# Convolution and routed experts on one core: blocks of 512 rows with seven products for eight, and whole sequences routed at once

## The chip, the cores and the metric

The kernel runs on one core of one Trainium2 chip. The metric is the device time of one execution in microseconds. Times of several runs are given as their median; one further execution is taken by the hardware profiler, and views of the profile come from that one. The engines are called TensorE (PE; its weight loads are PEld), VectorE (DVE), ScalarE (ACT), GpSimd (POOL) and SyncE (SP).

## The reference

A light convolution of 8 sequences of 3584 tokens with 192 channels (8 heads of 24, seven taps, softmax over the taps) feeds a mixture of 8 experts of width 1024. A token goes to the expert with its largest logit, unless a local gate says that it stays with the expert of the token before it, so the routing is a scan along the sequence:

```python
out = np.einsum('hk,bskhg->bshg', w, x_unf)          # causal, 7 taps
...
logits = np.einsum('bsd,de->bse', x, w_gate)
local_gate = 1.0 / (1.0 + np.exp(-np.einsum('bsd,de->bse', x, w_local).squeeze(-1)))
...
            if s == 0 or local_gate[b, s] < 0.5:
                e = fresh_e
            else:
                e = prev_e if prev_e >= 0 else fresh_e
...
            h = np.maximum(x[b, s] @ w1[e], 0.0)
            out[b, s] = p[e] * (h @ w2[e])           # p: softmax of the logits
```

Everything is fp32. Each token goes through one expert: a first product 192 to 1024, a relu, a second product 1024 to 192.

## The kernel before, in words

The 28,672 tokens are 16 groups of 1792 (`PT`), two groups to a sequence. Groups 0 and 1 take a path of their own at the start (`wide`, `wide_route`), on TensorE. A later group is loaded with its halo by `load_x` (one transfer of 1.9 MB on SP's queue), convolved on VectorE by `conv` (L366: per head one ACT scaling and six VectorE multiply-adds, L387, over 128 x 336 elements), and routed by `route` (L601): `logits` (L565) turns the rows on VectorE (L570) and multiplies on TensorE (L580), and some ninety small VectorE instructions find each token's expert and its slot in DRAM. `put` (L768) scatters 128 rows at a time to their slots with an indirect transfer on GpSimd's queue (L775).

The slots of an expert are units of 128 rows. `table` (L788) makes a list on the chip of units that are already full, and the static list `blocks` (L887) says which entry of which table a block takes: 35 blocks of one unit, 87 of two, 20 of one, and two spare ones at the end that are entered by a test on the chip. The caps `ONE` and `TWO` come from `_sure` (L48): only as many blocks are planned after a group as must be full whatever the routing.

A block loads its expert's weights (`load_w`, 1.5 MB, SP's queue, four buffers, three blocks ahead) and its rows (`load_rows`), turns the rows on TensorE into PSUM and copies them out on ACT (`turn`, L928, L949), and computes the first product with relu (`hidden`, L952; matmuls L963, ACT L968) and the second (`output`, L973; matmuls L980). The second product's sum is scaled by the token's probability on ACT (L988) and VectorE (L992), and an indirect transfer writes the rows to the output (L996). The contraction over 192 channels is cut into three pieces of 64 rows, and the width of 1024 into two halves, one in each half of TensorE's rows; an fp32 matmul of the code shows as two records.

The order of the work is written out by hand. The loop over `blocks` (L1138) issues for each block `hidden`, the turning of the next block's rows, `step`, `output`, `step`. `step(time)` (L1037) issues VectorE work of convolution and routing for about `time` microseconds by the costs that the generators yield. PSUM has four one-bank buffers for the first product, two for the second and one of two banks for the turned rows.

## Time and profile before

| | us |
|---|---|
| median of 3 runs | 1315.88 (1315.37 to 1316.42) |
| the profiled execution | 1326.81 |
| its span, first to last instruction | 1325.1 |
| TensorE busy (share of the span) | 1304.4 (98%) |
| VectorE busy | 778.3 (59%) |
| ACT busy | 625.2 (47%) |
| GpSimd busy | 480.4 (36%) |
| second product on TensorE, L980, 7328 records | 641.0 |
| first product on TensorE, L963, 6816 records | 637.2 |
| convolution on VectorE, L387, 672 instructions | 376.5 |
| moved by DMA | 325.29 MB |

A group of instructions is named by its line, engine and operation, with what it writes and reads; its busy time is the time in which at least one of its instructions ran, so overlapping matmuls are not counted twice. A wait is put down to the instruction that released it. The timeline gives the start and the length of runs of like instructions.

### The profile page before, as it was taken

The numbers are of one execution on the slowest core, as the hardware profiler recorded it, in microseconds if no ns is written. First come the engines' busy times: TensorE is split into PE (matmuls) and PEld (weight loads), VectorE is DVE, ScalarE is ACT, GpSimd is POOL, SyncE is SP. The second block draws the span as 40 slices with busy tenths as digits, with TensorE's granted clock in tenths as the row PEclk, the third lists the DMA queues.
The fourth block names the chain that finished last, engine by engine and source line by source line (L and its number), as shares of the span: only waits on it lengthen the run. The fifth ranks groups of instructions, "written<-read, shape, count | busy, mean of one in ns | idle before, by whom it ended". The sixth has DMA issues, their size and how long they took to land. (4 is left out here: it accounts for less than half of the span.)

```text
span 1325.1 us, 41356 instructions
## 1 busy us (share of the span) xinstructions
PE 1304.4 (98%) x16682; PEld 1260.9 (95%) x16682; DVE 778.3 (59%) x2434; ACT 625.2 (47%) x1571; POOL 480.4 (36%) x520
## 2 busy tenths in 40 slices
PE   9899999999999999999999999999999999999997
PEld 7799999999999999999999999999999999999997
DVE  6888898977878787878777878785610000000000
ACT  5345555544454545444545454544444444444553
POOL 4445352534343434343434343434344212211111
PEclk9999999999999999999999999999999999999999
DMA  5789999967575757575757575756565555556893
GB/s 188 283 349 391 376 365 345 394 213 266 182 275 177 290 188 277 201 260 192 271 186 273 193 271 199 267 195 210 197 211 205 189 185 188 192 187 229 313 317 131
DMA packets 67298, 325.29 MB, mean 245 GB/s; under 512 B 12576, under 2 KB 38103, under 8 KB 47650
## 3 DMA queue, kind: packets, MB, share of 16 engines
q1 hardware_dynamic: 44784, 277.41, 58.4%
q0 software_dynamic: 22320, 45.22, 9.2%
q8 instruction: 133, 2.18, 0.7%
q14 instruction: 59, 0.48, 0.1%
q10 hardware_dynamic: 2, 0.00, 0.0%
HBM read 277.29 MB, written 45.77 MB: 244 GB/s over the span
## 5 line engine op out<-in xcount | busy, mean ns | idle before, releaser
L980 PE MATMUL yps<-wb,hT 64*128 64x192 f32 x7328 | 641.0, 325 | 5.8 <-ACT hT L968 2.8
L963 PE MATMUL hps<-xT,wb 64*128 64x256 f32 (+1 forms) x6816 | 637.2, 336 | 1.7 <-issue 1.4
L963 PEld LDWEIGHTS hps<-xT,wb 64*128 64x128 f32 x6816 | 589.1, 187 | 27.2 <-issue 4.0
L980 PEld LDWEIGHTS yps<-wb,hT 64*128 64x128 f32 x7328 | 602.8, 187 | 11.1 <-issue 4.6
L996 POOL DMA_INDIRECT out_dram<-o_sb,xg x229 | 232.3, 1014 | 605.7 <-DVE o_sb L992 533.9
L968 ACT ACTIVATE hT<-hps 128x512 f32<-128x512 f32 (+1 forms) x568 | 261.9, 512 | 361.4 <-PE hps L963 246.5
L387 DVE SCALAR_TENSOR_TENSOR y_sb<-x_sb,c,y_sb 128x336 f32<-128x336 f32 x672 | 376.5, 570 | 18.9 <-issue 0.8
L992 DVE SCALAR_TENSOR_TENSOR o_sb<-yps,xg,o_sb 128x192 f32<-128x192 f32 x229 | 87.5, 414 | 467.8 <-ACT o_sb L988 461.4
L775 POOL DMA_INDIRECT slots<-y_sb,posi x228 | 231.2, 1014 | 209.3 <-ACT xT L949 114.8
L988 ACT ACTIVATE o_sb<-yps,xg 128x192 f32<-128x192 f32 x229 | 86.9, 418 | 289.8 <-PE yps L980 287.4
L949 ACT COPY xT<-xps 64x256 f32<-64x256 f32 (+4 forms) x568 | 210.8, 371 | 11.7 <-issue 1.7
L377 ACT ACTIVATE y_sb<-x_sb,c 128x336 f32<-128x336 f32 x112 | 63.7, 581 | 0.0
L359 PEld LDWEIGHTS xps<-ident,xg 64*128 64x128 f32 (+1 forms) x916 | 57.0, 124 | 5.2
L359 PE MATMUL xps<-ident,xg 64*128 64x64 f32 (+1 forms) x916 | 60.0, 217 | 0.0
L570 DVE STREAM_TRANSPOSE z<-y_sb 128x768 f32<-128x768 f32 (+1 forms) x56 | 45.4, 853 | 0.4
L596 DVE COPY lt<-lq 32x36 f32<-32x36 f32 x224 | 40.8, 182 | 3.5
L580 PE MATMUL hps<-z,wg 64*32 64x128 f32 x1344 | 24.2, 272 | 1.2 <-issue 1.2
L580 PEld LDWEIGHTS hps<-z,wg 64*32 64x32 f32 x1344 | 19.2, 105 | 4.1 <-issue 2.9
L556 PE MATMUL yps<-y_sb,hot 112*128 112x194 f32 x64 | 12.6, 353 | 1.4 <-DVE hot L550 1.1
L556 PEld LDWEIGHTS yps<-y_sb,hot 112*128 112x128 f32 x64 | 11.3, 202 | 2.1 <-DVE hot L550 1.6
L672 DVE COPY bk<-so_far 1x32 f32<-1x32 f32 x56 | 12.3, 220 | 0.7
L588 DVE STREAM_TRANSPOSE lq<-ls 128x256 f32<-128x256 f32 x14 | 6.2, 441 | 10.9 <-ACT ls L585 10.9
(236 smaller groups left out, 358.0 us busy)
## 6 DMA issues: line engine op xcount, KB each, us to landing
wb<-in_w_dram SPq DMA_DIRECT2D x138, 1536.0 KB
x_sb<-in_x_dram SPq DMA_DIRECT2D x14, 1920.0 KB
xg<-slots SPq DMA_DIRECT2D x87, 195.0 KB
wb<-in_w_dram SPq DMA_DIRECT2D x12, 512.0 KB
xg<-slots SPq DMA_DIRECT2D x53, 97.5 KB
out_dram<-o_sb,xg POOLq DMA_INDIRECT x229
slots<-y_sb,posi POOLq DMA_INDIRECT x228
x_sb<-in_xb_dram SPq DMA_DIRECT2D x4, 768.0 KB
```

What stands on the lines that cost most here:

```text
L359: nc.tensor.transpose(to, src[rows], identity=ident[rows, rows])
L377: nc.scalar.activation(cols(h), chans(h, 0), Act.Copy, scale=c[:, h, 0:1])
L387: nc.vector.scalar_tensor_tensor(cols(h), chans(h, k), c[:, h, k:k + 1], cols(h), Alu.mult, Alu.add)
L570: nc.vector.transpose(z[:, t:u, :], y_sb[:, t:u, Y0:Y0 + D])
L775: ins = nc.gpsimd.indirect_dma_start(out=slots[:, :], in_=rows, in_offset=None, out_offset=bass.IndirectOffsetOnAxis(ap=to, axis=0)).ins
L949: copied = nc.scalar.copy(a, b)
L963: nc.tensor.matmul(hps[half][:, j, w], lhsT=wb[rows, f0:f0 + P], rhs=xT[rows, d, w], start=(d == 0 and j == 0), stop=(d == KD - 1), skip_g ...
L968: relu = nc.scalar.activation(hT[:, m:m + 2, w], hps[half][:, :, w], Act.Relu)
L980: nc.tensor.matmul(yps[half][:, k * D:(k + 1) * D], lhsT=hT[rows, m, k * P:(k + 1) * P], rhs=wb[rows, WA + m * D:WA + (m + 1) * D], start= ...
L988: nc.scalar.activation(o_sb[:, k, :], y[k][0], Act.Copy, scale=xg[:, k, 0:1])
L992: nc.vector.scalar_tensor_tensor(o_sb[:, k, :], y[k][1], xg[:, k, 0:1], o_sb[:, k, :], Alu.mult, Alu.add)
L996: sent = nc.gpsimd.indirect_dma_start(out=out, in_=o_sb[:, k, :], in_offset=None, out_offset=bass.IndirectOffsetOnAxis(ap=xg.bitcast(I32)[ ...
```

## The change

**Blocks.** The static list becomes 51 blocks of one unit, 20 of two, 31 of four (512 rows) and 14 of one. A new estimate, `_likely`, plans blocks that are full for a routing as it is expected; where an entry of a table is not full, the block takes a unit of padding, and 28 spare blocks, in two nested tests, take what is then left.

**Seven products.** For a block of 512 rows the first product takes two of its three pieces of channels as a 2 x 2 by 2 x 2 block product (rows in halves of 256, the width in two halves) and forms it with Strassen's seven products (`seven`); the third piece is added with four plain ones. GpSimd forms the combined weights (`combine_w`, four subtractions of 128 x 256), VectorE the combined rows (`combine_x`, five), and partial sums go from PSUM through ACT copies and VectorE adds to `h11`, `h12`, `h21`, `h22`. The second product of such a block is done in two parts of 256 rows.

**Convolution and routing.** From group 4 on two groups, a whole sequence, are convolved and routed together (`GROUPS`, `NS`), and x lies by heads: a unit of convolution is one head of one group or sequence, with its own load (240 or 417 KB) on ACT's queue, begun by `taps` behind the scaling of the output.

**Logits.** The group of logits matmuls is cut in two, and the first half stands inside the second product of a block (`visit`), at the earliest one block after the turning; before, the whole group stood ahead of it.

**The rest.** Scatters hang behind other steps and one at a time, PSUM is cut in four pools of two banks, buffers of the start lie in a pool that is closed before the blocks, and the start has another order.

```diff
-ONE = [_sure(min(g + 1, EARLY) * PT, UT) for g in range(NPART)]
-TWO = [_sure((g + 1) * PT - ONE[-1] * UT, BT) if g >= EARLY else 0 for g in range(NPART)]
+def _likely(tokens, size, left):
+    return max(0, (tokens - left) // size)
...
+GROUPS = [*range(EARLY)] + [*range(EARLY + 1, NPART, 2)]
+ONE = {g: _sure((g + 1) * PT, UT) if g + 1 < EARLY else _likely(EARLY * PT, UT, LEFT1) for g in GROUPS}
...
+FOUR = {g: _likely((g + 1) * PT - PAST, QT, LEFT if g < LAST else LEFT3) if g + 1 >= FIRST else 0
+        for g in GROUPS}
...
+        x_sb = x_all[:, at:at + n + HALO, :]
+        src = x[g // PER, qq]
...
+        (queue or nc.scalar).dma_start(out=x_sb.rearrange("p t d -> p (t d)"), in_=win)
...
+            load_x(u)
+        for u in range(max(st["unit"], 0), st["unit"] + 4):
+            if u > st["unit"] and not ready(u, wait):
+                return
+            if u not in begun and most:
+                tap(u)
+                most -= 1
...
+        for k in range(1, KC):
+            nc.vector.scalar_tensor_tensor(cols, x_in[u][:, k:k + n, :],
+                                           c[:, h, k:k + 1], cols, Alu.mult, Alu.add)
+            yield 0.6 if n == NT else 1.0
...
+            for b in range(DQ):
+                if b == DQ // 2:
+                    yield "half"
...
+    def combine_x(xT):
+        xc = hp.tile([P, 4, HU * P], F32, name="xc")
+        one, two = slice(0, HU * P), slice(HU * P, KT * P)
+        nc.vector.tensor_tensor(xc[:, 0, :], xT[:, 0, one], xT[:, 0, two], op=Alu.subtract)
+        nc.vector.tensor_tensor(xT[:, 0, two], xT[:, 0, two], xT[:, 1, two], op=Alu.add)
...
+    def seven(wb, wt, xT, xc, turn_next, weights_next):
...
+        def times(to, a, b, first=False):
+            for j in range(2):
+                for half, rows in halves():
+                    ins = nc.tensor.matmul(to[:, half, j, :], lhsT=b[rows, j * P:(j + 1) * P],
+                                           rhs=a[rows, :], start=(first and j == 0), stop=True,
+                                           skip_group_check=True)
+            return ins
+
+        times(xb, a11, b11, True)
+        nc.scalar.copy(h11, xb)
+        times(yb, s1, t1, True)
+        times(yb, a23, b32)
+        nc.scalar.copy(h22, yb)
+        times(xb, s2, t2)
+        nc.scalar.copy(h12, xb)
+        put(times(wbk, a12, b21, True))
+        times(wbk, a13, b31)
+        step(SIDE[0], None, 1)
+        nc.vector.tensor_tensor(h11, wbk, h11, op=Alu.add)
+        nc.scalar.activation(h11, h11, Act.Relu)
+        put(times(xb, s3, t3))
+        nc.vector.tensor_tensor(h22, xb, h22, op=Alu.add)
+        nc.scalar.activation(h22, h22, Act.Relu)
+        times(yb, s4, b22)
+        put(times(yb, s5, b32))
+        at = turn_next()
+        times(xb, a22, t4)
+        wt = weights_next()
+        next(wt)
+        put(times(xb, a23, b31))
+        next(wt)
+        nc.vector.tensor_tensor(h12, yb, h12, op=Alu.add)
+        nc.scalar.activation(h12, h12, Act.Relu)
+        nc.scalar.activation(h21, xb, Act.Relu)
+        return [[h11, h12], [h21, h22]], at, wt
...
+    SIDE = (2.8, 4.4, 1.6, 1.4)
...
-    step(1.8)
-    xT, _ = turn(blocks[0][1], xgs[0])
-    gather(1, ya, picks[1], range(9, NB))
+    puts_behind(mark["rs", 1], 4)
+    at = turn_out(blocks[0][1], xgs[0])
+    xgs[1] = gathered(picks[1])
+    xT, _ = turn_in(blocks[0][1], at)
     next(route1)
-    puts_behind(mark["oh", 1], 2)
-    step(2.4)
-    xgs[1] = gathered(picks[1])
+    step(0.6)
```

## The prediction

> **What bounds the kernel now.** I read the busy table and the slices first, then TensorE's timeline in steady state, then the stretches, then the waits. In the page, the slices are busy tenths of each engine over 40 equal parts of the span:
>
> ```profile
> PE   9899999999999999999999999999999999999997
> DVE  6888898977878787878777878785610000000000
> PEclk9999999999999999999999999999999999999999
> DMA  5789999967575757575757575756565555556893
> ```
>
> TensorE is full from the second slice to the end at full clock; VectorE has nothing left to do after two thirds of it. DMA is full in slices 4 to 8. So TensorE's own work sets the time, and the question is what a block of it costs. Its timeline, start and length in us, first for blocks of 256 rows, then of 128, then with a logits group between:
>
> ```profile
> 1102.37 5.34 PE L963 MATMUL hps<-xT,wb 64*128 64x256 f32 x48
> 1107.55 0.39 PE L359 MATMUL xps<-ident,xg 64*128 64x64 f32 x8
> 1107.78 5.42 PE L980 MATMUL yps<-wb,hT 64*128 64x192 f32 x64
> 1113.03 5.34 PE L963 MATMUL hps<-xT,wb 64*128 64x256 f32 x48
> ...
> 1263.88 2.84 PE L963 MATMUL hps<-xT,wb 64*128 64x128 f32 x48
> 1266.56 0.28 PE L359 MATMUL xps<-ident,xg 64*128 64x64 f32 x4
> 1266.67 2.82 PE L980 MATMUL yps<-wb,hT 64*128 64x192 f32 x32
> 1269.33 2.84 PE L963 MATMUL hps<-xT,wb 64*128 64x128 f32 x48
> ...
> 329.95 0.56 PE L359 MATMUL xps<-ident,xg 64*128 64x64 f32 x8
> 330.44 1.59 PE L580 MATMUL hps<-z,wg 64*32 64x128 f32 x96
> 331.96 5.74 PE L980 MATMUL yps<-wb,hT 64*128 64x192 f32 x63
> ```
>
> From start to start: a 256-row block takes 10.66 us (48 records at 107.9 ns, 8 transposes at 28.8, 64 records at 82.0); each fp32 matmul of the code is two records. A 128-row block takes 5.445. The logits group starts 0.26 after the transposes' 0.23 us are over and holds TensorE until 331.96: 1.78 us.
>
> The stretches (busy us and, in brackets, instructions; then clock, DMA share, GB/s) show where TensorE is not full:
>
> ```profile
> 50.00:100.00 50.00, 45.48 (x727) 43.38 (x726) 41.63 (x130) 25.44 (x80) 22.39 (x23) 1.00 0.82 314
> 100.00:150.00 50.00, 48.55 (x789) 47.02 (x788) 44.61 (x117) 27.10 (x84) 25.40 (x26) 1.00 1.01 399
> 150.00:200.00 50.00, 49.58 (x749) 48.94 (x748) 44.59 (x145) 27.51 (x88) 20.99 (x20) 1.00 0.95 356
> 1000.00:1100.00 100.00, 100.00 (x1134) 93.87 (x1134) 6.68 (x18) 42.98 (x96) 27.23 (x28) 1.00 0.57 198
> ```
>
> The ledger from the starts of the blocks: the 35 single blocks run 46.16 to 260.09, 213.9 us, against 35 x 5.445 + 4 logits x 1.78 = 197.7 of work: 16.2 lost, 5.5 of it in the first four blocks, 10.7 (0.34 each) in the other 31, where DMA stands at 0.95 to 1.01 [...]. The 87 pairs run to 1208.90, 948.8 us against 927.4 + 10 x 1.78: 3.6 lost. The last 20 singles lose 0.5. The wait table agrees: TensorE's own named waits come to some 13 us, ACT's, VectorE's and GpSimd's to hundreds, which cost nothing while TensorE is full.
>
> [...]
>
> **The change part by part.** Which blocks run follows from the constants: before 35 singles, 87 pairs, 20 singles; after 51 singles, 20 pairs, 31 fours, 14 singles. Both are 229 units of 128. Routing the reference's own inputs by its own rule gives 229 units and fills each planned block, so neither the two spare units of before nor the 28 of after are entered, and no block of padding runs.
>
> 1. Strassen. A block of 512 is 11 calls of `times`, each 4 matmuls or 8 records of 256 columns: 88 x 107.9 = 9.50 us; 16 transposes 0.46; second product 128 x 82.0 = 10.50. Sum 20.46, against 2 x 10.66 = 21.32: 0.86 less, x31 = **-26.7 us**.
> 2. Five pairs become ten singles: 54.45 - 53.3 = **+1.15**.
> 3. Logits: still 14 groups of 96 records, each now in two halves: [...] 14 x 0.26 = **+3.6**. [...]
> 4. The single stage is 16 longer at the same appetite for weights (1.5 MB per 5.445 us is 289 GB/s, rows in and out add 36, x and scatters the rest of the 355 to 399 measured). At 0.34 each: 16 x 0.34 = +5.4. In front of it the two slices of convolution (1.8 and 2.4) leave VectorE's path to `oh` and `upto`, and block 2's rows, whose scatters end at 52 now, can be fetched some 2 us sooner: -2. Together **+3.3**; from -8 (loads of 240 KB in place of one of 1.9 MB no longer collide with weights) to +15 (twice the loss).
> 5. Stalls inside a block of 512. Its eviction is a chain TensorE, ACT, VectorE, TensorE. I price ACT from its rows (256 elements 381 ns, 512 595, so 1024 about 1.02 us) and VectorE's add from `oh` (112, 275 ns) and `hot` (512, 691): 1024 about 1.22, an estimate with a PSUM operand taken at the same rate. From the block's start: call 1 ends 0.86, ACT copies h11 to 2.1, h22 to 3.85, h12 to 4.9; call 7 wants that bank at 5.2: 0.25 spare. VectorE adds h11 5.4 to 6.6, h22 6.6 to 7.8; the call after the transposes wants it at 8.23: 0.3 spare. h12 is ready at 10.4 for 12.6, h21 at 11.4 for 15.2. Behind the ACT copies stand o_sb's scalings and the taps, behind the adds the convolution slices of VectorE, whose five subtractions for the next block (5 x 0.425) end at 19.1 and are wanted at 21.3. So the margins hold but thinly: 0 to 0.9 a block, I take 0.15: +4.7. The 20 pairs lose 0.8; before lost 3.6. Net **+1.9**.
> 6. The first block of 512 has its weights combined in a row and its rows after that: once, **+1.5** (0 to 3).
>
> Costed at nothing: convolution by heads. VectorE's rows give 192 elements 414 and 336 elements 570 ns, so 672 about 0.93: 96 x 0.57 + 288 x 0.93 = 323 us against 376.5; routing two groups at once saves more, the adds and subtractions cost 31 x 5.8 = 180. VectorE ends near 810 us busy, in a block of 512 about 17.7 of 20.46 (10.2 of planned slices, 5.8, four scalings 1.7); the cover is TensorE's time, and without it each us late shows. GpSimd per block of 512: 4 sends, 6 scatters at 1.0 and 4 subtractions of some 0.75 are 13 of 20.5. ACT issues x's loads, 64 of them (SP's take 0.33 us); in a single block ACT has the second half of TensorE's time free, and relu waits if a tap and a load come together. Where the scatters were spread, they still wait on TensorE's or ACT's steps; GpSimd alone waits. The gathers' buffers, the pools opened anew and the tables touch no engine at its limit. The tail after the last matmul, 1318 to 1325, stays.
>
> Sum: -26.7 + 1.15 + 3.6 + 3.3 + 1.9 + 1.5 = -15.2. The profiled execution took 1326.81 with a span of 1325.1; the span becomes 1309.9. It was 0.8% above the median of the runs, 1315.88; I carry the difference over: **1300.7**.
>
> **The rivals.** (a) The front clears: small x loads leave the weights on time, the single stage loses 8 in all and blocks of 512 nothing. That is 11.5 and 4.7 better than my sum, less what the pairs lose anyway: about 1287. For it: half of the loss sits where a 1.9 MB load ran. Against: 399 GB/s is the measured ceiling, and it is reached for 50 us. (b) Slower: the chain in the block of 512. If call 7 waits for ACT's copy and the call after the transposes for VectorE's add, 0.45 each, a block loses 0.9 and not 0.15: 31 x 0.75 = +23, 1324. It decides from 0.64 a block on. For it: spare times of 0.25 and 0.3 in two strict queues that carry other work; against: the work ahead in them is sliced to end before. (c) The DMA front is worse: at 0.66 a single the 47 later blocks lose 31, not 16: 1316, no change. For it: share 1.01 already; against: x's halo shrinks from 20/14 to 34/28 of the rows. (d) The seven products do not save TensorE time, if 44 matmuls go slower than 48[...].
>
> **How the numbers follow.** Mine 0.52 (1294 to 1308), (a) 0.20 (1284 to 1294), (c) 0.15 (1308 to 1318), (b) 0.13. Within 0.2% is 1313.3 to 1318.5, about what a measurement can tell from no change. Faster: 0.52 + 0.20 + half of (c) = 0.80; same 0.07; slower 0.13. The range 1287 to 1319 leaves out most of (b) and the best of (a).
>
> **What would show it.** Right: blocks of 512 start 20.5 to 20.8 us apart, with 88 records near 108 ns; the first block of 256 starts near 350 us; 28 logits bursts. Wrong: idle of TensorE before the first product named after ACT's copies or VectorE's adds (b); single blocks 6 us apart with DMA at 1.0 (c); singles at 5.45 throughout (a). Blocks of 512 above 21.3 apart would overturn the forecast.

## The result, and the profile after

| | before | after |
|---|---|---|
| median of the runs, us | 1315.62 (1314.50 to 1316.42) | 1330.73 (1325.88 to 1331.05) |
| the profiled execution, us | 1326.81 | 1330.98 |
| its span | 1325.1 | 1329.3 |
| TensorE busy | 1304.4 | 1285.1 |
| VectorE, ACT, GpSimd busy | 778, 625, 480 | 821, 691, 618 |
| moved by DMA, MB | 325.29 | 281.17 |

The changed kernel is slower: the ratio is 1.0107, with an interval of 1.0082 to 1.0131. The forecast was 1300.7, so it went the other way. TensorE is busy for 19 us less, and still the end comes later. (A set is the runs that were made together; the same program before took 1315 us in four of the six sets and 1329 to 1332 in the other two, so times are compared within a set only.)

The page of the changed kernel, the slices of the span that answer to those shown of before:

```profile
PE   8879999999899999989999999899999999999997
DVE  6857888789678898885788955853333334333100
PEclk9999999999999999999999999999999999999999
DMA  4888999989877678664434434335334333233483
```

Before, TensorE's row was 9 in slice 1 and from the third slice on. Now it has an 8 in slice 1, a 7 in slice 3, and 8s in slices 11, 18 and 26, and VectorE's row has gained work to the end. The DMA row is at 8 or 9 from slice 2 to 11, where before has that from 3 to 8, and far emptier behind. The wait table of TensorE in the same execution (releaser, us in total, times, longest) names what the gaps wait for:

```profile
PE ps L400 <- DVE h L1140: 8.1, 3, 3.5
PE ps L1170 <- DVE o_sb L1186: 7.6, 2, 5.9
PE ps L1170 <- ACT h L1078: 3.8, 1, 3.8
PE ps L1125 <- DVE xT L1103: 3.2, 2, 2.6
PE ps L400 <- DMA xg<-slots: 3.1, 1, 3.1
```

Four of the five releasers are VectorE or ACT. The prediction had put the waits inside a block at 4.7 us in all and the convolution on VectorE at nothing. A block of 512 without a wait is as predicted; the timeline of TensorE (start, length) has:

```profile
886.20 10.58 PE L1170 MATMUL ps<-wb,h 64*128 64x192 f32 x128
896.60 2.77 PE L1125 MATMUL ps<-xT,wb 64*128 64x256 f32 x24
...
904.37 0.65 PE L400 MATMUL ps<-ident,xg 64*128 64x64 f32 x16
...
906.62 0.67 PE L1170 MATMUL ps<-wb,h 64*128 64x192 f32 x6
```

From second product to second product 906.62 - 886.20 = 20.42 us; the prediction had 20.46. Of the 30 distances from one such block to the next, 20 are 20.41 to 20.43 us, and seven, where logits stand or VectorE is busy with routing, 20.5 to 23.5. Most of the loss is in three blocks: the first (25.96), the second (23.04) and the thirteenth, at 846.78 (29.40). The thirteenth waits twice for VectorE, as TensorE's timeline shows, and VectorE's has routing (L912) right up to the add (L1140) that ends the second wait:

```profile
850.42 2.00 PE L1125 MATMUL ps<-xT,wb 64*128 64x256 f32 x16 [2.58 <-DVE xT L1103]
861.09 0.69 PE L400 MATMUL ps<-ident,xg 64*128 64x64 f32 x16 [3.49 <-DVE h L1140]
```

```profile
859.67 0.23 DVE L912 SCALAR_TENSOR_TENSOR inn<-ends,pf,inn 128x8 f32<-128x8 f32 x1
859.82 1.22 DVE L1140 TENSOR_TENSOR h<-ps,h 128x1024 f32<-128x1024 f32 x1
```

The ledger by stages, from the starts of the blocks in this execution. Work is blocks times their undisturbed length (5.445, 10.66, 20.42) and half logits bursts at 1.09:

| stage | starts, us | took | work | lost | lost, as predicted |
|---|---|---|---|---|---|
| before the first block | 0 | 42.98 | | | 46.2 at the start, as before |
| 51 singles | 42.98 | 318.5 | 290.8 | 27.7 | 19.6 (16.2 + 5.4 - 2) |
| 20 pairs | 361.46 | 222.3 | 221.9 | 0.4 | 0.8 |
| 31 of 512 | 583.77 | 659.8 | 641.7 | 18.1 | 6.2 |
| 14 singles | 1243.6 | 76.3 | 76.2 | 0 | 0.5 |
| tail behind the last matmul | 1319.86 | 9.4 | | | 6.8 |

In the front, the loss is not spread over the singles. 33 of the 51 take 5.44 or 5.45 us from start to start, and of the other 18 six hold the two half bursts of a group of logits; the loss is at a few places. The first twelve singles lose 18.4 of the 27.7 us, and the last one, at the handover to the pairs, 5.2. Two of the places, in the timelines of ACT and then TensorE:

```profile
69.20 0.34 ACTq L156 DMA_DIRECT2D x_sb<-in_x_dram  x1
...
80.27 0.58 ACT L425 ACTIVATE y_sb<-x_sb,c 128x336 f32<-128x336 f32 x1 [5.21 <-DMA x_sb<-in_x_dram]
80.75 1.18 ACT L1078 ACTIVATE h<-ps 128x256 f32<-128x256 f32 x4
...
85.49 0.36 ACTq L156 DMA_DIRECT2D x_sb<-in_x_dram  x1
...
95.77 0.58 ACT L425 ACTIVATE y_sb<-x_sb,c 128x336 f32<-128x336 f32 x1 [5.79 <-DMA x_sb<-in_x_dram]
...
96.38 0.42 ACT L1180 ACTIVATE o_sb<-ps,xg 128x192 f32<-128x192 f32 x1
```

```profile
77.08 0.31 PE L400 MATMUL ps<-ident,xg 64*128 64x64 f32 x4
81.17 4.26 PE L1170 MATMUL ps<-wb,h 64*128 64x192 f32 x32 [3.78 <-ACT h L1078]
...
88.16 2.87 PE L1170 MATMUL ps<-wb,h 64*128 64x192 f32 x32
...
99.75 5.20 PE L1170 MATMUL ps<-wb,h 64*128 64x192 f32 x32 [5.93 <-DVE o_sb L1186]
```

ACT stands at a scaling of x (L425) whose load is still under way, and the relu (L1078) and the scaling of the output (L1180) stand behind it in ACT's queue; TensorE waits for these. Counted in the order of the loads, the first scaling needs the one issued at 69.20, the second the one at 85.49: 11.1 and 10.3 us for 240 KB. The lengths in TensorE's lines show a second price: 32 records take 4.26 and 5.20 us behind the two stalls and 2.87 without one.

### The profile page after: what moved, and what is told of

Read it like the earlier page. It is cut to its first block, busy times and chain, and to the rows that moved or that the text cites. A ratio compares the mean times of both kernels' runs of the same rounds, so it can differ in the third digit from the quotient of the medians.

```text
span 1329.3 us, 40917 instructions
## 1 busy us (share of the span) xinstructions
PE 1285.1 (97%) x16674; PEld 1237.7 (93%) x16674; DVE 821.3 (62%) x1891; ACT 691.1 (52%) x1402; POOL 618.4 (47%) x650
## 2 busy tenths in 40 slices
DMA packets 67395, 281.17 MB, mean 212 GB/s; under 512 B 12544, under 2 KB 33207, under 8 KB 52866
## 4 chain that ended last, share of the span: by engine, by line
PE 50%; DVE 3%; ACT 1%; issue 0%; POOL 0%; POOLq 0%; DVEq 0%; ACTq 0%
PE ps L1170 26%; PE ps L1125 20%; PE ps L1074 3%; PE ps L400 1%; DVE y_sb L461 1%; PE ps L662 1%; ACT xT L1052 0%; DVE h L1143 0%; DVE o_sb L1186 0%; DVE h L1140 0%; DVE h L1153 0%; ACT h L1154 0%; ACT h L1134 0%; ACT y_sb L425 0%; ACT h L1136 0%
## 5 line engine op out<-in xcount | busy, mean ns | idle before, releaser
L1170 PE MATMUL ps<-wb,h 64*128 64x192 f32 x7328 | 632.3, 326 | 11.8 <-DVE o_sb L1186 7.6
L1170 PEld LDWEIGHTS ps<-wb,h 64*128 64x128 f32 x7328 | 603.4, 189 | 17.1 <-ACT xT L1052 7.9
L461 DVE SCALAR_TENSOR_TENSOR y_sb<-x_sb,c,y_sb 128x672 f32<-128x672 f32 (+1 forms) x384 | 321.9, 847 | 52.8 <-ACT y_sb L425 42.7
L1074 PE MATMUL ps<-xT,wb 64*128 64x128 f32 (+1 forms) x4080 | 295.3, 297 | 3.4 <-issue 1.9
L1074 PEld LDWEIGHTS ps<-xT,wb 64*128 64x128 f32 x4080 | 275.6, 188 | 16.6 <-issue 3.7
L1186 DVE SCALAR_TENSOR_TENSOR o_sb<-ps,xg,o_sb 128x192 f32<-128x192 f32 x229 | 87.2, 410 | 274.3 <-ACT o_sb L1180 273.0
L1180 ACT ACTIVATE o_sb<-ps,xg 128x192 f32<-128x192 f32 x229 | 87.3, 418 | 312.4 <-PE ps L1170 311.1
L1078 ACT ACTIVATE h<-ps 128x256 f32<-128x256 f32 (+1 forms) x340 | 128.6, 431 | 146.0 <-PE ps L1074 119.5
L1052 ACT COPY xT<-ps 128x128 f32<-128x128 f32 (+2 forms) x464 | 194.1, 418 | 9.8 <-PE ps L400 3.2
L1125 PE MATMUL ps<-xT,wb 64*128 64x256 f32 x1488 | 179.9, 379 | 3.2 <-DVE xT L1103 3.2
L1125 PEld LDWEIGHTS ps<-xT,wb 64*128 64x128 f32 x1488 | 154.1, 189 | 10.2 <-issue 3.9
L1140 DVE TENSOR_TENSOR h<-ps,h 128x1024 f32<-128x1024 f32 x31 | 37.9, 1222 | 77.4 <-PE ps L1125 77.3
L1125 PE MATMUL ps<-xc,wt 64*128 64x256 f32 x496 | 64.8, 376 | 0.0
L425 ACT ACTIVATE y_sb<-x_sb,c 128x672 f32<-128x672 f32 (+1 forms) x64 | 50.8, 796 | 18.2 <-DMA x_sb<-in_x_dram 14.9
L1125 PE MATMUL ps<-xc,wb 64*128 64x256 f32 x496 | 59.2, 376 | 0.0
L400 PE MATMUL ps<-ident,xg 64*64 64x64 f32 (+1 forms) x916 | 47.4, 218 | 11.1 <-DVE h L1140 8.1
L400 PEld LDWEIGHTS ps<-ident,xg 64*64 64x64 f32 (+1 forms) x916 | 42.7, 123 | 16.3 <-DVE h L1140 9.3
```

The source lines that it names most:

```text
L400: nc.tensor.transpose(to, src[rows], identity=ident[rows, rows])
L425: nc.scalar.activation(got[g][:, :, Y0 + h * GS:Y0 + (h + 1) * GS], x_in[u][:, :n, :], Act.Copy, scale=c[:, h, 0:1])
L461: nc.vector.scalar_tensor_tensor(cols, x_in[u][:, k:k + n, :], c[:, h, k:k + 1], cols, Alu.mult, Alu.add)
L1052: copied = nc.scalar.copy(a, b)
L1074: nc.tensor.matmul(hps[:, half, j, :], lhsT=wb[rows, f0:f0 + P], rhs=xT[rows, d, :], start=(d == 0 and j == 0), stop=(d == KD - 1), skip_g ...
L1078: relu = nc.scalar.activation(hT[two][:, half], hps[:, half], Act.Relu)
```

## The experiments

**Set 1: the kernels again, and two single edits.** The first two runs are the unchanged kernels.

> The kernel before, unchanged, for a profile of it at its usual time: the one shown took 1326.81, the timed runs 1315.6. If the 11 us lie in the single blocks, [...] the first block of 256 rows starts near 249 and not at 260.09; if they are spread, all blocks are longer.

> The changed kernel, unchanged: 1326 to 1331. If its stalls are fixed by its order, TensorE's waits for ACT's relu near 81 us, for VectorE near 100 and near 861 are there again, within 1 us of the lengths 3.8, 5.9 and 3.5; if they come from chance in the transfers, they move or go.

Before took 1326.11 us (one run; the set's other runs of it have a median of 1329.36), with its first 256-row block at 259.89: no execution near 1315 was seen in this set, so the question stayed open. The changed kernel took 1357.76, ratio 1.0205 (1.0176 to 1.0234). Its stalls are at the same places: blocks of 512 of 25.96, 24.63 and 29.40 us (first, second, thirteenth), ACT's late scalings with TensorE stalls of 4.83 and 5.13 in the first twelve singles. That is the order of the work. What is larger is above all the single stage, 333.3 us against 318.5. The second block, 24.63 here and 23.04 before, is taken up in the last section.

```diff
-        if st["unit"] + 1 == len(UNITS) and st["cgen"] is None:
-            time *= 1.6
```

> The factor of 1.6 on each slice of VectorE's side work after the last convolution is taken out; nothing else. Theory of the queues (routing slices are issued ahead of the adds that TensorE waits for): the block that starts near 847 falls from 29.3 us to 20.4, and the time by 8 to 9 us, to 1322. Rival (the blocks of 512 wait for something else, such as transfers): the block stays long and the time within 2 us of 1330.7.

Measured 1353.57, 1.0180 (1.0152 to 1.0208) beside 1.0205: 3 to 4 us for the 8 to 9 expected, and the two intervals overlap. The thirteenth block does fall from 29.40 to 20.42 us, as expected. But the last group is now routed later, and another wait takes its place, in TensorE's timeline of this kernel:

```profile
1014.56 1.94 PE L1125 MATMUL ps<-xc,wb 64*128 64x256 f32 x16
1022.50 1.12 PE L400 MATMUL ps<-ident,xg 64*128 64x64 f32 x16 [6.00 <-DMA xg<-slots]
```

The block that turns here is the first that needs rows of the last two groups. The stretch paid 9 us early for rows in time; without it 6 us come back later, with longer records behind them (the eight that take 2.05 us take 1.14 in the changed kernel's second block of 512, at a granted clock of 1.00).

```diff
-        if st["cgen"] is None and ready(st["unit"] + 1):
+        if st["cgen"] is None and ready(st["unit"] + 1, 3 if st["block"] < 21 else 1):
```

> In the first 21 blocks a convolution unit may begin three blocks after its load was issued, not one; no work is taken out. Theory of the queues (ACT stands at a scaling whose x has not landed, and the relu behind it is late): the ACT waits of 5.2 and 5.8 us and TensorE's of 3.8 and 5.9 go, and the time falls by 10 to 15 us, to 1318. Rival (weights and x are short of bandwidth whatever waits for them): TensorE waits as long for weights, time within 3 us of 1330.7.

Measured 1357.92, 1.0211 (1.0185 to 1.0236): no gain, the rival's number. Yet the rival's reason is not what the trace shows. ACT's waits for x fell from 10.8 us to 3.5 and both stalls in the first twelve singles are gone; the stage of single blocks is 322.7 us against 333.3 in the run beside it. The time came back as TensorE waiting for rows, 8.9 us in three places, one of them in the pairs:

```profile
494.80 0.69 PE L400 MATMUL ps<-ident,xg 64*128 64x64 f32 x8 [4.29 <-DMA xg<-slots]
```

VectorE may start each unit only later, so routing, scatters and then rows are late; that this is the way from the edit to the late rows is read from the order of the work and was not tested apart. Here the wait moved off ACT came back as a wait for rows.

**Set 2: which part of the change loses.** Before takes 1314.84 in this set. The changed kernel itself was not run in it: where before takes 1315 it was at 1.0107 in the result and at 1.0047 in set 3, so a gain or loss of a few us beside it can't be read from the times of this set.

```diff
-        times(xb, a11, b11, True)
-        nc.scalar.copy(h11, xb)
...
+        def three(to, parts, weights):
+            for k in range(3):
+                ins = times(to, parts[k], weights[k], k == 0)
+            return ins
...
+        three(xb, lefts, ones_)
+        nc.scalar.activation(h11, xb, Act.Relu)
+        put(three(yb, lefts, twos_))
+        nc.scalar.activation(h12, yb, Act.Relu)
```

> The changed kernel with the first product of a block of 512 as twelve plain products (96 records in place of 88), without the combined weights and rows and without VectorE's adds: each quarter of h is made by one ACT relu from PSUM. Same output. By the prediction's first step a block costs 8 x 107.9 ns = 0.86 us more, 26.7 us over 31 blocks; but the stalls that wait for VectorE's adds and subtractions (some 15 us in the changed kernel's blocks of 512) should go. Theory, both hold: 8 to 15 us slower than the changed kernel on the same chip (1357.8 there), blocks 21.3 us apart, stage of blocks of 512 near 672 us. Rival, the stalls come from the convolution's place in VectorE's queue and stay: 22 to 27 us slower. Rival, the seven products' helpers (adds, subtractions, copies) take back all they save: within 3 us.

1335.58, 1.0165 (1.0148 to 1.0182). In the timeline the first product of such a block is one unbroken run of 96 records:

```profile
865.57 10.53 PE L1104 MATMUL ps<-xT,wb 64*128 64x256 f32 x96
875.92 0.63 PE L400 MATMUL ps<-ident,xg 64*128 64x64 f32 x16
```

A block takes 21.28 us, 0.86 more than 20.42, exactly the 8 x 107.9 ns of the prediction. The 31 blocks take 668.0 us (580.32 to 1248.32), which is 31 x 21.28 and the logits with nothing lost. So both halves of the theory hold: the seven products save 26.7, and the 18.1 lost in the changed kernel's blocks belong to what they need from the other engines. The edit takes out VectorE's part, GpSimd's and ACT's copies together; it is the wait table that names VectorE. The net gain of the seven products as made is 668.0 - 659.8 = 8 us.

```diff
-FIRST = 8
-PAIRED = 20
+FIRST = 16
+PAIRED = 99
```

> The changed kernel without blocks of 512: 51 blocks of one unit, 81 of two, 16 of one. Same output. What is left of the change is its front, its convolution by heads, the sequences routed whole and the logits in halves. Theory: the blocks of 512 do gain, 26.7 less some 17 of stalls, so this is 8 to 15 us slower than the changed kernel and 35 to 45 above the kernel before on this chip (1329), all of it in the single blocks, the logits and the tail. Rival, blocks of 512 are where the loss is: at least 5 us faster than the changed kernel.

1345.79, 1.0220 (1.0173 to 1.0267), beside 1.0047 to 1.0107 for the changed kernel where before takes 1315. The rival falls: blocks of 512 are no net loss. What stays of the change without them costs some 30 us.

```diff
-PAIRED = 20
+PAIRED = 28
...
-ONE = {g: ... else _likely(EARLY * PT, UT, LEFT1) for g in GROUPS}
+ONE = {g: ... else _sure((EARLY - 1) * PT, UT) for g in GROUPS}
-BT, LEFT2)) if g >= EARLY else 0
+BT, LEFT2)) if g >= EARLY else 8 if g == EARLY - 1 else 0
```

> The changed kernel with the 16 single blocks of group 3 made into 8 pairs: 35 singles, 28 pairs, 31 blocks of 512, 14 singles. Same output; 8 loads of weights of 1.5 MB fewer in the front. Theory A, the loss in single blocks is a loss per single ([...] 42 us over 51 in the changed kernel on this chip, 28 on the other): 16 x 0.5 to 0.8 plus 8 x 0.23 of work = 10 to 15 us faster than the changed kernel on the same chip. Theory B, the loss is at two places in the first twelve singles (x landing late for ACT) and at the handover: 2 to 5 us faster.

1335.63, 1.0146 (1.0121 to 1.0170): no faster, contrary to both theories. (The profiled execution, 1342.05, is the slowest of its four.) But it speaks against theory A. The 35 singles now take 222.0 us (43.17 to 265.15), 22.7 more than their work, and 19.2 of these lie in the first twelve, as 18.4 do in the changed kernel. The loss is not per single. The eight pairs behind them then run into a wait that the wait table puts first:

```profile
PE ps L400 <- DMA xg<-slots: 14.8, 1, 14.8
PE ps L400 <- DVE h L1140: 6.4, 3, 2.9
PE ps L1170 <- DVE o_sb L1186: 6.2, 1, 6.2
```

The rows of groups 4 and 5 come at 362, when all blocks made of the first four groups are done. In the changed kernel the same rows come at 357. TensorE can't pass that point early, whatever the front saves, for a whole sequence must be convolved, routed and scattered first.

```diff
-    for u in range(4):
+    for u in range(6):
         load_x(u, nc.sync)
...
-        for _ in range(most):
+        for _ in range(2):
             u = len(x_in)
```

> The changed kernel with x loaded earlier: six units ahead of the first block in place of four, and up to two loads per single block in place of one (no more than six in flight, as now). Same output and same bytes. Theory B, x arrives at one unit per single block while VectorE could convolve 1.4, so ACT's scalings wait for x and what stands behind them is late: ACT's waits for x go, TensorE's two stalls of 4 to 6 us near 80 and 100 us go with the slow clock after them; 8 to 15 us faster than the changed kernel on the same chip. Theory A, the transfers themselves are the limit: the same bytes land no sooner, weights come late in their place; within 3 us.

1324.80, 1.0072 (1.0052 to 1.0093). The 8 to 15 us that were expected are not shown, since the changed kernel's own 1.0047 to 1.0107 lie on both sides. Beside the kernel with twelve products, which has the changed kernel's front and ran in this set, the single stage is 3.0 us shorter, 311.1 for 314.1. The stall near 100 us (1.9 us there, 5.9 in the result's execution) is gone, the one near 80 stands with 3.1, and the handover still waits 3.6 us for rows. ACT's scalings wait 4.9 us for x by name, and 5.9 us are put down to transfers of weights (4.5 of it at the scaling near 80). Theory B holds in kind and not in size: the same bytes, begun earlier, end part of the waits.

**Set 3: the mends together.** Before takes 1315.60.

> The changed kernel as it is, for the comparisons of this set: 1.1% above the kernel before on a chip where that takes 1315, as in the result; stalls at the same places in the blocks of 512 (first block 25.9 us, second 23.0, the block near 847 us 29.3), since these come from the order of VectorE's work and not from the transfers. Rival, the places shift: then the stalls are chance meetings.

1322.52, 1.0047 (1.0030 to 1.0063), and not the 1.1% that was expected. The stalls in the blocks of 512 are where they were, 25.83, 23.03 and 29.25 us: no chance meetings. Those of the front are at their places too, near 80 and 97 us, but at 2.8 and 2.4 us they are shorter than the result's 3.8 and 5.9, and the single stage is 312.6 us for 318.5. So the loss in the blocks of 512 repeats, and the loss in the front does not have a fixed size.

```diff
-PAIRED = 20
-LEFT1 = 640
+PAIRED = 19
+LEFT1 = 384
-LEFT = 2900
+LEFT = 1876
...
-        for _ in range(most):
+        for _ in range(2):
...
-        if st["unit"] + 1 == len(UNITS) and st["cgen"] is None:
-            time *= 1.6
...
-    for u in range(4):
+    for u in range(6):
...
-            if spot and part == 0:
-                taps(min(n, 2), 2 if n == 1 else 1)
+            if spot is not None and part == 0:
+                taps(min(n, 2) if spot else 0, 2 if n == 1 else 1)
...
-        if n < KT:
+        if n < KT and not n < n_next == KT:
             step(1.4 if n == 1 else 3.6)
```

> The changed kernel with what the runs so far name: six units of x loaded ahead and two per block (7 us in the run with earlier loads); 53 single blocks and 19 pairs in place of 51 and 20, so that the first pair comes 10.7 us of work later and finds its rows (5 us less at the handover, 0.2 more work); no convolution step at the end of the last pair block, but its loads of x (3 to 7 us of the 8 in the first two blocks of 512); no stretched steps after the last convolution, with two more blocks of 512 planned ahead of the last group so that its rows are not wanted at once (8 us, and not the 6 us wait for rows of the run without the stretch alone). Theory, each stall has its own place and cause: the sum is -18 to -27, 1304 to 1313 where before takes 1315. Rival, a stall that is removed comes back elsewhere, as in the two runs with one edit each: -7 to -10, the earlier loads' own gain.

1301.70, 0.9894 (0.9877 to 0.9910) of before, 20.8 us under the changed kernel in the same set. The 31 blocks of 512 take 641.7 us (571.87 to 1213.61): their work and nothing else. That is 17.8 of the 25.7 by which the two profiled spans of this set differ (1324.2 and 1298.6). The single stage takes 316.7 for 53 singles, 6.8 less than the changed kernel's 312.6 plus the 10.9 of two more; and TensorE's named waits are now

```profile
PE ps L1170 <- ACT h L1078: 3.3, 1, 3.3
PE ps L1170 <- DVE o_sb L1186: 1.6, 2, 1.0
PE ps L1170 <- ACT xT L1052: 1.5, 1, 1.5
...
PE ps L400 <- DMA xg<-slots: 0.8, 1, 0.8
```

No line of a block of 512 is left (L1125, or L400 behind L1140). The rival, that each stall comes back elsewhere, falls: this time the rows of the last group are planned for two blocks later when its routing is no longer hurried.

```diff
-                if b == DQ // 2:
-                    yield "half"
...
-            st["bank"], st["due"], st["half"] = bank, False, True
+            st["bank"], st["due"] = bank, False
...
-        if spare[SPARE:]:
-            with left(spare[SPARE:]):
-                also(spare[SPARE:])
```

> The changed kernel with each logits group in one piece at the place where its first half stood, and with only the first two spare blocks behind the list (26 of the 28 left out, which these inputs never enter). Theory: half bursts of 1.09 us twice against one of about 1.8, 0.4 x 14 = 5.6 us; the tail behind the last matmul falls from 9.4 to the 6.8 of before, 2.6 us; sum 6 to 8 us faster than the changed kernel. Rival: the second half is free of the output's path only because it is short, and a whole group of 96 records makes ACT or VectorE wait for banks: within 3 us; or the tail is longer for another reason than the nested spare blocks and stays above 9.

1324.42, 1.0054 (1.0037 to 1.0071): no gain over 1.0047. The two parts can be read apart in the trace. The tail is 6.7 us, against 9.2 beside it: the nested spare blocks cost 2.5, as the theory had it. A whole logits group takes 1.7 to 1.9 us in its block where two halves take 2.15 (22.30 and 22.14 us against 22.59 and 22.56 for the same two blocks of 512), so 14 groups could give 4 to 6. But the first two blocks take 26.91 and 24.71 for 25.83 and 23.03. Their stalls have not grown (2.91 and 1.66 us for 2.92 and 1.65); the records are longer: the mean granted clock of the execution is 0.989 for 0.991 beside it, and the records of one of the products (ps<-xT,wt) take 416 ns on average, for 408 in the changed kernel's first profile and 391 in the mended version, whose blocks of 512 have no stall. And a stall in the front grows from 2.4 to 4.6. So the halves' cost is confirmed in size and its removal didn't reach the end.

The last edit of this set is made to the mended version:

```diff
-        if st["cgen"] is None and ready(st["unit"] + 1):
+        if st["cgen"] is None and ready(st["unit"] + 1, 3 if st["block"] < 21 else 1):
...
-                taps(min(n, 2) if spot else 0, 2 if n == 1 else 1)
+                taps(min(n, 2) if spot else 0, (3 if st["block"] < 21 else 2) if n == 1 else 1)
```

> The version with the four mends, and x used at the earliest three blocks after its load in the first 21 blocks (two for the scaling on ACT and one for the convolution before). Theory, what is left at 80 us is ACT standing at a scaling whose x is 10 us on its way: TensorE's stall of 3 us near 80 and the slow clock after it go, 3 to 6 us faster than the four mends alone. Rival, VectorE then has less to do early, routing slips and rows come late: no gain, a wait for rows in its place, as when only this edit was made.

1319.50, 1.0026 (1.0016 to 1.0036): 18 us slower than the mends alone, more than the rival said. The stall of 3.3 near 80 is gone, and the first line of the wait table is the rival's:

```profile
PE ps L400 <- DMA xg<-slots: 12.5, 5, 4.4
```

**Sets 4 and 5: one mend alone, before in both kinds of set, and the mended version again.** In set 4 before takes 1332.35.

> The kernel before, to see a profiled execution of it that is near its median. The prediction took a span of 1325.1 us, 11 us above the median of the runs, and carried the difference over to the changed kernel. If the 11 us lie in the single blocks (transfers), the first block of 256 rows starts near 249 us in an execution of 1315 and at 260 in one of 1326, and everything behind it takes the same time. Rival: the profiler itself adds it, all along the span; then each profiled execution is 0.8% above the others, and the first block of 256 rows stays at 258 to 260.

Median 1331.46, profiled 1330.28: the profiler adds nothing, so the rival falls. The first 256-row block starts at 264.60, and the pairs take 947.7 us, as in the execution that the prediction read (948.8).

```diff
-        if n < KT:
+        if n < KT and not n < n_next == KT:
             step(1.4 if n == 1 else 3.6)
```

> The changed kernel without the convolution step (3.6 us planned) at the end of the last pair block, ahead of the first block of 512; no other mend. Theory, VectorE's first add of the block stands behind nine slices of convolution: with four of them gone the first block takes 20.5 to 22 us and not 25.9. The second block (23.0) lacks a scaling of x issued ahead, since the last pair block loads no x: it stays at 22 to 23. Together 4 to 5.5 us faster than the changed kernel. Rival: the block waits for something that starts with the blocks of 512 itself [...]: within 1 us.

1353.97, 1.0159 (1.0107 to 1.0212); the time is that of a slow front (334.0 us of singles) and doesn't tell. The blocks do: the first of 512 takes 20.74 us, the second 23.16. VectorE's timeline of the changed kernel around its first block of 512, which begins at 583.77:

```profile
584.47 1.86 DVE L461 SCALAR_TENSOR_TENSOR y_sb<-x_sb,c,y_sb 128x672 f32<-128x672 f32 x2
586.25 0.73 DVE L1186 SCALAR_TENSOR_TENSOR o_sb<-ps,xg,o_sb 128x192 f32<-128x192 f32 x2
586.90 6.52 DVE L461 SCALAR_TENSOR_TENSOR y_sb<-x_sb,c,y_sb 128x672 f32<-128x672 f32 x7
593.35 1.22 DVE L1140 TENSOR_TENSOR h<-ps,h 128x1024 f32<-128x1024 f32 x1
```

and of this run, whose block begins at 608.89:

```profile
609.61 1.86 DVE L461 SCALAR_TENSOR_TENSOR y_sb<-x_sb,c,y_sb 128x672 f32<-128x672 f32 x2
611.38 0.74 DVE L1186 SCALAR_TENSOR_TENSOR o_sb<-ps,xg,o_sb 128x192 f32<-128x192 f32 x2
612.04 2.70 DVE L461 SCALAR_TENSOR_TENSOR y_sb<-x_sb,c,y_sb 128x672 f32<-128x672 f32 x3
614.80 1.23 DVE L1140 TENSOR_TENSOR h<-ps,h 128x1024 f32<-128x1024 f32 x1
```

Nine slices of convolution before the first add (L1140), or five: the add starts 9.58 us into the block, or 5.91. The prediction's chain had VectorE's add at 5.4. The theory holds and the rival falls. The second block stays long, as expected; in it VectorE's slices and the first add stand behind a scaling of x on ACT that the last pair block had not prepared, and in the mended version, which loads x there, it takes 20.42 us.

> The mended version once more, in another set, since the kernel before took 1315 in some sets and 1330 in others and the changed kernel 0.5 to 2.1% more. Theory, the four mends take away waits that come from the order of the work: blocks of 512 again lose nothing (642 us for 31), and the version stays 0.9 to 1.2% under the kernel before in either kind of set. Rival, its single blocks depend on the transfers as those of the changed kernel do: in a set where before takes 1330 it is within 0.5% of it.

> The kernel before in the same set as the mended version. If the set is a fast one (1315), its first block of 256 rows starts near 249 us; if a slow one (1330), at 260 to 265, and the pairs take 948 us in both.

In set 5 before takes 1315.17 and the mended version 1300.75, 0.9889 (0.9873 to 0.9906); its blocks of 512 take 641.7 again. Whether the gain holds where before takes 1330 is not shown: no run of it fell in such a set. The execution of before is at last one of 1314.35, and its timeline has the first 256-row block (L963) at

```profile
248.72 1.59 PE L580 MATMUL hps<-z,wg 64*32 64x128 f32 x96
250.25 5.45 PE L963 MATMUL hps<-xT,wb 64*128 64x256 f32 x48
```

10 us sooner than the 260.09 of the execution that the prediction read. Its pairs take 946.7, its singles 206.3. So of the 12.5 us between these two spans 7.6 lie in the single blocks, 2.2 ahead of them and 2.1 in the pairs.

## Why the prediction was wrong, by its steps

The predicted span was 1309.9, the measured one 1329.3: 19.4 more. The rest of the miss of 30 us, 10.6, is the difference between profile and median that was carried over. By the ledger, the blocks of 512 lose 11.9 more than predicted and the singles 8.1, the tail is 2.7 longer and logits cost 2.0 more; the start is 3.2 shorter, and the seven products and the other stages give back 2.1. That is the 19.4.

**Step 1, Strassen, held.** 20.42 us for 20.46, and 0.86 saved a block (twelve products beside seven, and the mended version without a stall). The rates of a record, 107.9 ns at 256 columns and 82.0 at 192, come from the trace. **Step 2 held**, with 5.445 a single. **Step 3 held nearly**: a group in halves costs 2.15 to 2.18 us in its block against 1.84 whole (12.50 - 10.66 in before), 0.3 to 0.35 for the predicted 0.26 (the pause ahead of a whole group in the trace of before), some 1 us in all (2 at most, with the 1.78 that the prediction took for a whole one).

**Steps 5 and 6 and what was costed at nothing failed, and cost 12 us of the 19.** "0 to 0.9 a block, I take 0.15" spreads the loss evenly; it was 0 in most blocks and 2.6 to 9 in three. The chain inside a block was priced rightly (the add 1.22 us, as estimated; the copies 1.01 for 1.02), and "the work ahead in them is sliced to end before" is the sentence that fell. It isn't so where one kind of block hands over to another. At the end of the last pair block a convolution step of 3.6 us is still issued, ahead of a step of 2.8 and the first add. In the second block no x is prepared. In the thirteenth, the stretch of the steps behind the last convolution puts the routing of the last sequence ahead of the subtractions and the adds; VectorE's table instructions fill the time up to 859.82 us, at which the first add starts. VectorE was 62% busy over the span, and by the prediction's sum 17.7 of 20.46 in the average block: the average cover was there, the order was not. Step 6 named the right block for a wrong reason (weights and rows instead of the slices in VectorE's queue), at 1.5 for 5.5.

**Step 4, the front, failed in its model and by 8 us in its sum.** "At 0.34 each" took the loss as one per single, with DMA at 0.95 to 1.01. (The 399 GB/s that rival (a) calls a ceiling are only the highest rate that it read in the trace of before: a slice of the changed kernel has 404.) But 33 of the 51 singles lose nothing. The loss is where ACT stands at a scaling for x, whose small load then takes 10 to 11 us, in the first twelve singles, and at the handover to the rows of groups 4 and 5. The sentence "relu waits if a tap and a load come together" named the mechanism and priced it at nothing; it should have asked how long a load takes where DMA is at 1.0 (11.1 us), and what is queued behind its user on ACT. The 2 us taken for rows fetched sooner are not shown either way: the start is 3.2 us shorter than in the execution that was read, but it varies from 44.0 to 46.4 us in the executions of before and from 43.0 to 46.3 in those of the changed kernel.

**The tail "stays"** was 9.4 for 6.8. Leaving out the nested spare blocks brings it to 6.7 where the changed kernel beside it has 9.2: here the skipped code cost 2.5 us at the end.

**Carrying the profile's 11 us over was a wrong step by itself.** The execution of before that was read was one of 1326 us, with 16.2 lost in its singles; one of 1314.35 loses 206.3 - 35 x 5.445 - 4 x 1.78 = 8.6 there. The singles of before vary from execution to execution. The changed kernel was measured where before took 1315, and its own profiled execution is at its median. Against that lighter execution (span 1312.6), the changed kernel loses 19 us more in its singles, 18.1 in its blocks of 512 and 2.7 in the tail: 40 against the 28 that its blocks save (31 x (21.32 - 20.42)). With steps 2 and 3 (1.2 and 5.6, by the bursts of the ledger, 14 x (2.18 - 1.78)) and 2 us gained at the start and in the pairs that makes the 16.7 measured.

**The rivals.** (b) has the right sign, half the loss (8 us over before, measured 15) and the right pair of engines; its mechanism, each block a little late, is not what happened. (c), twice the loss in every single, is refuted in its form by the 33 that lose nothing, though its stage and nearly its size are right: the 47 later singles lose 23.5, where the forecast had 16 and (c) 31, and ACT's waits for x, 5.21 and 5.79 us, end with transfers. Half of (a) comes true with the mends, for blocks of 512 then lose nothing; the singles still lose 15.0, where (a) had 8. That the mended version's 1301.70 and 1300.75 meet the forecast's 1300.7 is luck: it is another kernel, with less loss than the forecast had, and the forecast set out from a slower execution. (d) is refuted by the runs: a block takes 20.42 us with 88 records and 21.28 with 96.

What stays open: why before's single stage takes 206 us in some executions and 214 to 218 in others, and the changed kernel's 313 to 333. It is not the chip alone, for one chip gave 1315.60 for before in set 3 and 1329.36 in set 1, another 1314.84 in set 2 and 1332.35 in set 4. Only the loads' place in time was varied, not the load on the memory. The stall near 80 us wasn't removed without a new wait.

## What to carry to other kernels

Where an engine's work is hidden behind another's, check the order in its queue at each place where the pattern changes (the first block of a new kind, the last slice of the background work), not only its busy share over an average block; a stall there costs its length and, for five of the eight stalls of over 1.5 us behind the start of the first block in the changed kernel, 3.4 us or more at a clock of 0.50. A background load whose user stands in one queue with work of the critical path has to be planned with the time that the trace shows for it, here 10 to 11 us at a DMA share of 0.84 to 1.01, and not with its size; using it later instead, as two runs did, only moved the wait to the rows. Before a profile's distance from the median is carried over to another kernel, ask which stage it lies in.

## What the runs showed of the hardware

**A stall can be paid for twice.** Three stretches of the changed kernel, one before and two behind the stall of 5.93 us (the window and its length, busy us and instructions of PE, PEld, DVE, ACT and POOL, then the granted clock, DMA share and GB/s):

```profile
90.83:93.70 2.87, 2.87 (x55) 2.83 (x52) 0.00 (x0) 0.00 (x0) 0.94 (x1) 1.00 0.98 385
99.70:102.50 2.80, 2.75 (x18) 2.78 (x20) 2.73 (x5) 0.00 (x0) 2.03 (x2) 0.50 0.83 339
102.50:105.00 2.50, 2.50 (x23) 2.50 (x21) 0.68 (x2) 0.01 (x1) 0.94 (x1) 0.60 0.31 95
```

The clock was at 0.50, and 0.60 is the mean of a stretch in which it returned. The changed kernel's execution has five such stretches between its first block and its last. Four are 3.41 us long, from 80.62, 357.10, 596.03 and 862.27 us, with stalls of 3.78, 3.07, 2.92 and 3.49; the one here, from 97.69, is 6.83 long, with the stall of 5.93. Behind stalls of 2.58 us (thirteenth block, from 850.42) and 1.65 (second) the clock stayed at 1.00. The length of the stall alone does not decide in these traces: in the profile of before, an idle time of 2.00 us that ended at 41.06 was followed by 0.50 from 42.99 to 46.40, and the stall in the second block of 512 was once followed by long records and once not. In the changed kernel of the result, and then in its repetition in set 1, that block has:

```profile
619.35 0.69 PE L400 MATMUL ps<-ident,xg 64*128 64x64 f32 x16 [1.65 <-DVE h L1140]
620.57 1.14 PE L1125 MATMUL ps<-xT,wt 64*128 64x256 f32 x8 [0.53 <-DVE h L1143]
621.50 1.06 PE L1125 MATMUL ps<-xT,wb 64*128 64x256 f32 x8
```

```profile
641.42 0.69 PE L400 MATMUL ps<-ident,xg 64*128 64x64 f32 x16 [1.66 <-DVE h L1140]
642.64 2.08 PE L1125 MATMUL ps<-xT,wt 64*128 64x256 f32 x8 [0.53 <-DVE h L1143]
644.48 1.73 PE L1125 MATMUL ps<-xT,wb 64*128 64x256 f32 x8
```

The stalls are the same. In the first the granted clock is 1.00 (619.35 to 624.00), and the block takes 23.04 us; in the second eight records take 2.08 and the next eight 1.73 us, near the 1.93 and 1.98 of those at 0.50 in the first block of 512, and the block takes 24.63, 1.6 more. With slow records behind the stall the first block of 512 is 5.5 us longer for 3.5 us of idle (2.92 and 0.53) and the thirteenth 9.0 for 6.6; the second, without them, 2.6 for 2.2. No step of the prediction had this term.

**VectorE beside GpSimd.** The sums and differences of rows (L1102 to L1106) take 0.42 us in most blocks, and three of the five 0.83 to 0.95 in front of the first block of 512, where GpSimd makes its four subtractions in a row at the same time (580.66 to 583.93 us). In the mended version GpSimd's four come at 568.86 to 572.38 us, and the three slow ones (0.83 to 0.94) fall beside them there, L1104 to L1106. L1103 (569.64 to 570.06) falls beside them too and takes 0.42, but GpSimd's subtraction that begins with it (569.67) takes 0.97, where the other three take 0.74 to 0.79. The price in the changed kernel is a doubling of three instructions, some 1.3 us; its cause was not tested apart.

**A small load in a full system.** 240 KB took 11.1 us from issue to use at a DMA share of 1.01 and 10.3 at 0.84 (at the two scalings that waited); a load issued at 104.99 us, where the share had just been 0.31, was used after 4.4, and over these the share was 0.87. So the share alone does not tell the time. At the 388 GB/s moved during the 11.1 us the bytes alone are 0.6 us. With x on ACT's queue and the weights on SP's no slice of the page has more than 404 GB/s, where before, with both on SP's, none had more than 394: 10 GB/s more in the fullest slice. What the other queue does to that was not tested apart.
